# A chunked scan before a routed expert layer: another order of PE's products in a step, decay in another PSUM bank, routing in five groups

## The chip, the cores and the metric

The kernel runs on one core of a Trainium2 chip. The metric is the device time of one execution in microseconds, the median of several runs. A core has five engines that run side by side and wait for each other through semaphores: PE (matrix products into PSUM), DVE (vector), ACT (scalar functions and copies), POOL (general, and here the indirect DMAs), and SP, which here only issues DMAs. "PEld" is PE's loading of the stationary operand, which the profile lists by itself.

## The reference

Two stages. The first is a state-space scan over 4 batches x 8 heads x 768 positions, with head size 32 and state size 16:

```python
for c in range(nc):
    cum = np.cumsum(la, axis=-1)
    L = np.exp(cum[:, :, :, None] - cum[:, :, None, :]) * causal
    M = np.einsum('bhin,bhjn->bhij', Cc, Bc) * L
    y_intra = np.einsum('bhij,bhjd->bhid', M, xc)
    y_inter = np.einsum('bhin,bhnd->bhid', Cc, state) * np.exp(cum)[:, :, :, None]
    y[:, :, sl] = y_intra + y_inter
    state = decay_full[:, :, None, None] * state + np.sum(Bx, axis=2)
```

The second takes the result as 3072 tokens of 256 numbers, gives each token to the best of 8 experts (top 1 of a product with a gate matrix), and computes there `relu(x @ w1[e]) @ w2[e]`, times the gate's probability.

## The kernel before, in words

The scan works on chunks of 64 positions, two batches at a time: 24 chunks ("steps"), in two runs of 12, each run beginning with an empty state. The program is written out by hand, one loop over n from 0 to 25 at its end, and each engine does its instructions in the order in which that loop issues them. In step n the work of three chunks is under way: chunk n (its decay matrix L and its scores), chunk k = n - 1 (its state and its output y), chunk j = n - 2 (its output turned into token rows). The pieces:

- `decay(n)`: DVE's scan gives L from `abc`, a PSUM tile that `a_rows(n)` fills by one full-size product.
- `scores(n)`: 8 products of 32 rows x 64 columns into the tile g; `weigh(n)`: DVE multiplies g by L, giving M.
- `scaled_B(n)`: POOL scales B by L's last column, giving bs.
- `own(k)`: 8 products of 64 x 32 into the bank A, the chunk's part of the state; `fade(k)`: ACT scales the carried state (Sd); `state(k)`: DVE adds the two to the new state S.
- `decay_in(n + 2)`: 3 full-size products (128 x 128, bf16), copied by ACT to dec; `decayed_C(n + 2)`: POOL multiplies it with C, giving ctd.
- `y(k)`: 8 products of 32 x 64 of ctd with the carried state (y<-ctd,S), then 16 of 64 x 32 of M with x (y<-M,xn), into the tile y; ACT copies it to yT.
- `rows(j)`: full-size products of yT with an identity and the gate weights, into the tile rows_ps (tokens and their gate scores), copied by ACT.
- `masks(g)`: ACT spreads C for four chunks ahead.

An fp32 product counts as two PE instructions in the profile.

Routing works on groups of chunks (`RGS`). The first `GA` groups, 17 chunks together, are the first pass; the last 7 chunks are placed during the expert phase. When the rows of a group are complete, its choice is made in stages that later steps carry out (`due`): stage 0 `choose_max` (largest score), stage 1 `choose` (one-hot of the expert) and `count` (POOL), stage 2 `rank_pe` (small full-size products on PE that number the tokens) and `rank` (DVE). The bank of rank_pe is that of rows_ps. Then `place(k)`, an indirect DMA on POOL's queue, scatters a chunk's rows into an array in DRAM, sorted by expert; one chunk a step, from the list `todo`. `empty_consts` prepares a tile of empty rows (zrows) that SP writes behind the tokens in step 21.

At step 23 SP issues the reading of the first two experts' tokens, which waits for all scatters of the first pass. Then follow the experts: h (first product, relu on ACT), y_ps (second product), scaled and scattered to the output. Loads of inputs and of the first experts' weights are issued by SP behind counted numbers of PE products.

The order of PE in step n is: own, decay_in, rank_pe (if due), the two parts of y, scores, a_rows, rows.

Of the kernel before, what the change touches and what calls it, by code (L numbers as in the profile page):

```python
# [9 lines left out]
FP32 = mybir.dt.float32  # L10
# [11 lines left out]
CH = 64  # L22
# [4 lines left out]
NG = NT // CG  # L27
RGS = [2, 3, 3, 3, 3, 3, 7]
GA = 6
R0 = [sum(RGS[:i]) for i in range(len(RGS))]  # L30
# [14 lines left out]
def ssd_then_moe(ctx, tc, x, ad_in, az_in, B, BT, CT, w_gate, w1, w2, out):  # L45
# [94 lines left out]

    def empty_consts():

        z = sm.tile([128, 1], FP32, name="zero")
        nc.gpsimd.memset(z, 0.0)
        none_i = sm.tile([112, CAP // 112], I32, name="none_i")
        nc.gpsimd.iota(none_i, pattern=[[0, CAP // 112]], base=N, channel_multiplier=0)
        nc.scalar.copy(zrows, bc(z[0:112, 0:1, None], list(zrows.shape)))
        nc.gpsimd.tensor_copy(zrows[:, :, TOK].bitcast(I32), none_i)

    iota_i = sm.tile([128, E], I32, name="iota_i")  # L150

# [23 lines left out]
    def mm(out, lhsT, rhs, **kw):  # L175
        i = nc.tensor.matmul(out, lhsT=lhsT, rhs=rhs, **kw)  # L176
        passes[0] += 2 if rhs.dtype == FP32 else 1
        if batches and passes[0] >= 99 + 253 * sent[0] // 2:
            sent[0] += 1
            for send in batches.pop(0):  # L180
                d = send()
                tc.add_manual_dep(d.ins, i.ins.name,
                                  mybir.DependencyInfo(mybir.DependencyClass.Sync, mybir.DependencyReason.DATA),
                                  reason="behind the entry of a block")

    def empty(e):
# [99 lines left out]

    def masks(g, uu=(0, 1)):

        if "ctm" not in gr[g]:
            gr[g]["ctm"] = wk.tile([128, CG, 2, 2, CH], FP32, name="ctm")  # L290
        m = gr[g]["ctm"]
        for u in uu:
            nc.scalar.mul(m[:, :, :, u, :], gr[g]["CT"].rearrange("p (c s i) -> p c s i", c=CG, s=2), par[:, u:u + 1])  # L293

# [28 lines left out]
    def state_bank(k):  # L323

        if "A" not in st[k]:
            st[k]["A"] = ps.tile([128, 2, 128], FP32, name="A", bufs=1)
        return st[k]["A"]

    def decay_in(ns, bank):
# [33 lines left out]
    def scaled_B(n):  # L363
        if n % NC == NC - 1:
            return
        nc.gpsimd.tensor_tensor(out=bs[n % 2], in0=gr[n // CG]["B"][:, n % CG].rearrange("p (h m) -> p h m", h=8),  # L366
                                in1=bc(st[n]["L"][:, :, CH - 1:CH], [128, 8, NS]), op=ALU.mult)

    def scores(n):
        c = n % CG  # L370
        g = ps.tile([128, 2, 512], FP32, name="g", tag="g", bufs=1)
        for s in range(2):
            for t in range(2):
                for v in range(2):
                    r = slice(64 * t + 32 * v, 64 * t + 32 * v + 32)
                    o = c * 128 + s * CH
                    mm(g[64 * t:64 * t + 64, v, 128 * s:128 * s + 128],
                                     lhsT=gr[n // CG]["BT"][r, o:o + CH],
                                     rhs=gr[n // CG]["ctm"][r, c, s].rearrange("p u i -> p (u i)"),
                                     start=(s == 0), stop=(s == 1), skip_group_check=True)  # L380
        st[n]["g"] = g
# [11 lines left out]
    def own(k):  # L393
        if k % NC == NC - 1:
            return
        A = state_bank(k)
        xk = gr[k // CG]["x"][:, k % CG]

        for s in range(2):
            for t in range(2):  # L400
                for v in range(2):
                    r = slice(64 * t, 64 * t + 64)
                    h = 4 * s + 2 * v
                    mm(A[32 * (2 * t + v):32 * (2 * t + v) + 32, 0, 64 * s:64 * s + 64],
                                     lhsT=bs[k % 2][r, h:h + 2].rearrange("p u m -> p (u m)"),
                                     rhs=xk[r, h * D:(h + 2) * D], start=(s == 0), stop=(s == 1),
                                     skip_group_check=True)
# [11 lines left out]
    def state(k):  # L419
# [3 lines left out]
        new = wk.tile([128, 2, 2 * D], FP32, name="S", bufs=3)  # L423
        A = st[k]["A"][:, 0].rearrange("p (s d) -> p s d", s=2)
        for u in range(2):
# [9 lines left out]
    def y(k):  # L435
        p = ps.tile([128, 2, 512], FP32, name="y", bufs=1)
        inter = k % NC > 0
        xk = gr[k // CG]["x"][:, k % CG]
        if inter:
            for s in range(2):  # L440
                for t in range(2):
                    for v in range(2):
                        r = slice(64 * t + 32 * v, 64 * t + 32 * v + 32)
                        o = s * CH
                        mm(p[64 * v:64 * v + 64, t, s * CH:s * CH + CH], lhsT=carry[k][r, s],
                                         rhs=st[k]["ctd"][r, o:o + CH], start=(s == 0), stop=False,
                                         skip_group_check=True)
        for s in range(2):
            for q in range(4):
                for t in range(2):  # L450
                    r = slice(64 * t, 64 * t + 64)
                    o = (4 * s + q) * D
                    mm(p[D * q:D * q + D, t, s * CH:s * CH + CH], lhsT=xk[r, o:o + D],
                                     rhs=st[k]["M"][r, 4 * s + q], start=(not inter and s == 0), stop=True,
                                     skip_group_check=True)
        st[k]["yT"] = wk.tile([128, 2, 128], FP32, name="yT")
        nc.scalar.copy(out=st[k]["yT"], in_=p[:, :, 0:128])  # L457
# [4 lines left out]

    def rows(k, bank):

        p = ps.tile([128, DM + E], FP32, name="rows_ps", tag=bank, bufs=1)
        for t in range(KT):
            mm(p[:, 128 * t:128 * t + HB], lhsT=st[k]["yT"][:, t], rhs=turn[:, HB * t:HB * t + HB],
                             start=(t == 0), stop=(t == KT - 1), skip_group_check=True)
        g = grp[k]
        nc.scalar.copy(out=rt[g][:, k - R0[g], 0:DM + E], in_=p)  # L470

# [7 lines left out]
    def choose_max(g):  # L479
        n = RGS[g]  # L480
        lg = rt[g][:, :, 128:HB]
        sh = [128, n, E]
        mx = route.tile([128, RG], FP32, name="mx")[:, 0:n]
        nc.vector.tensor_reduce(mx, lg, axis=AX, op=ALU.max)
        sub = route.tile([128, RG, E], FP32, name="sub")[:, 0:n]
        nc.vector.tensor_tensor(out=sub, in0=lg, in1=bc(mx[:, :, None], sh), op=ALU.subtract)

        eq = route.tile([128, RG, E], FP32, name="eq")[:, 0:n]
        nc.vector.scalar_tensor_tensor(out=eq, in0=sub, scalar=0.0, in1=bc(rev_e[:, None, :], sh),
                                       op0=ALU.is_equal, op1=ALU.mult)  # L490
        rt_v[g] = eq

    def choose(g):
        n = RGS[g]
        sl = slice(R0[g], R0[g] + n)
        eq = rt_v[g]
        m2 = route.tile([128, RG], FP32, name="m2")[:, 0:n]
# [54 lines left out]
    def place(k):  # L552
# [8 lines left out]
        else:  # L561
            tc.declare_no_dep(s_.ins, group="la",
                              reason="places of the second pass lie behind the rows that the first one reads")
            tc.add_to_no_dep_group("pb", s_.ins)


# [212 lines left out]
    with tc.manual_schedule():  # L779
# [19 lines left out]
        late_consts(hs)  # L799
        todo, due = [], {}  # L800
        for n in range(0, NT + 2):
# [4 lines left out]
            if n < NT:  # L806
                decay(n)
            if 0 <= k < NT:
                fade(k)
                own(k)  # L810
                if n > 1 and n + 2 < NT:
                    decay_in([n + 2], state_bank(k)[:, 1:2])
                for stage, q in jobs:
                    if stage == 2:
                        rank_pe(q, ps.tile([128, RG + 1, E], FP32, name="rank", tag="rows", bufs=1))
                state(k)
                y(k)
            for stage, q in jobs:
# [8 lines left out]
            if n < NT:  # L827
                scores(n)
                scaled_B(n)
                if n > 1 and n + 2 < NT:  # L830
                    decayed_C([n + 2])
                if n + 1 < NT:
                    a_rows(n + 1)
                weigh(n)

                if c in (1, 2) and g + 1 < NG:
                    masks(g + 1, (c - 1,))
                if n in act_jobs:
                    act_jobs[n]()
                if n == 12:  # L840
                    empty_consts()
            if 0 <= j < NT:
                if n == NT + 1:
                    keep_on()
                rows(j, "A" if n == NT + 1 else "rows")
                q = grp[j]
# [3 lines left out]
                if j == R0[q] + RGS[q] - 1:  # L850
                    if q < GA:
                        for i, d in enumerate((1, 2, 3) if q == 0 else (1, 1, 2)):
                            due.setdefault(n + d, []).append((i, q))
# [19 lines left out]
            if todo:  # L873
                place(todo.pop(0))
            for stage, q in jobs:
# [157 lines left out]
```

## Time and profile before

| what | us |
| --- | --- |
| median of 3 runs | 270.06 (268.4 to 270.72) |
| the profiled execution, its own time | 271.81 |
| its span, first to last instruction | 270.0 |
| scan, from the first L (7.05) to the last rows product (about 81.2) | 74 |
| expert phase, from its first h product (83.20) | to the end |

PE's mean granted clock is 0.992. A line of the windows gives a stretch of time and the busy time of each engine in it; a line of the chain gives a start, a duration, and the work that the end of the program hung on at that time; a line of the timeline gives start, duration from the first to the last of the instructions that it merges, engine, line of the program, operation, output and inputs, number, and in brackets how long its engine stood idle before it and what ended that. "issue" there is a wait that the profile shows no cause for.

A busy PE need not be a PE at its peak, since the ends of its products are modelled. What separates two products is better read from their starts.

### The profile page before, as it was taken

To read this page: it belongs to the slowest core of one execution; us is meant where nothing else is said; L and a number is where in the kernel's file an instruction comes from. 1 tells how busy PE (TensorE), PEld (TensorE's weight loads), DVE (VectorE), ACT (ScalarE), POOL (GpSimd) and SP (SyncE) were. 2 spreads that over 40 slices of the span, in tenths; PEclk is the share of its full clock that TensorE was granted. 3 is DMA by queue.
4 is the path that set the end of the run, shared out by engine and by line. 5 is a ranking of instruction groups with operands and counts; after the bars stand their busy time and mean duration, and the time that the engine had idled before them with its cause. 6 is when DMAs were issued, how large, how long until landed. Compare 5 with 4: busy or idle time off the path is not lost.

```text
span 270.0 us, 7603 instructions
## 1 busy us (share of the span) xinstructions
PE 252.9 (94%) x3044; PEld 213.7 (79%) x3067; DVE 110.7 (41%) x358; ACT 104.5 (39%) x304; POOL 87.0 (32%) x171
## 2 busy tenths in 40 slices
PE   8799898999997999999999999999999999999990
PEld 2577677677776888888888888888998978989770
DVE  4889887888854240421211111233225115321010
ACT  6958574655543423223232323141050520604200
POOL 5666875866720002025504120202211102121021
PEclk9999999999999999999999999999999999999996
DMA  6956767671434899949695959533330601401010
GB/s 182 374 172 171 228 199 236 165 247 51 135 118 101 212 367 310 384 177 294 236 256 202 279 199 335 130 91 78 103 85 9 94 4 30 90 6 40 2 35 28
DMA packets 29715, 43.57 MB, mean 161 GB/s; under 512 B 16203, under 2 KB 19917, under 8 KB 27984
## 3 DMA queue, kind: packets, MB, share of 16 engines
q1 hardware_dynamic: 27152, 36.32, 45.4%
q0 software_dynamic: 2496, 6.41, 7.1%
q8 instruction: 36, 0.59, 0.9%
q14 instruction: 31, 0.25, 0.3%
HBM read 29.10 MB, written 10.73 MB: 147 GB/s over the span
## 4 chain that ended last, share of the span: by engine, by line
PE 82%; DVE 5%; DMA 4%; issue 4%; POOL 2%; ACT 1%; POOLq 0%; ACTq 0%; DVEq 0%
PE h_ps L685 33%; PE y_ps L720 30%; PE y L176 5%; PE rows_ps L176 4%; PE g L176 3%; PE A L176 3%; PE yh_ps L731 3%; DVE L L359 2%; DMA x_hbm<-rows,pos 1%; DMA xs<-x_hbm 1%; DMA az<-in_az_dram 1%; DMA ct<-in_CT_dram 1%; DVE M L386 1%; PE rank L176 1%; DVE S L431 1%
## 5 line engine op out<-in xcount | busy, mean ns | idle before, releaser
L685 PE MATMUL h_ps<-xT,w 128*128 128x256 f32 (+3 forms) x516 | 90.3, 334 | 0.6 <-ACT xT L641 0.5
L685 PEld LDWEIGHTS h_ps<-xT,w 128*128 128x128 f32 x516 | 81.3, 190 | 8.2 <-ACT xT L641 0.7
L720 PE MATMUL y_ps<-w,hT 128*128 128x256 f32 x384 | 84.9, 380 | 0.0
L720 PEld LDWEIGHTS y_ps<-w,hT 128*128 128x128 f32 x384 | 72.6, 190 | 10.5 <-issue 0.8
L696 ACT ACTIVATE hT<-h_ps 128x256 f32<-128x256 f32 (+3 forms) x128 | 43.3, 339 | 60.8 <-PE h_ps L685 53.1
L711 POOL DMA_INDIRECT out_dram<-yo,xs x24 | 23.7, 988 | 91.1 <-ACT yo L703 64.7
L553 POOL DMA_INDIRECT x_hbm<-rows,pos x24 | 24.4, 1015 | 20.6 <-DMA x_hbm<-zrows 13.3
L359 DVE TENSOR_TENSOR_SCAN L<-abc,ident 128x512 f32<-128x512 f32 x24 | 29.1, 1213 | 0.0
L651 DVE COPY pl<-xs 128x256 uint16<-128x256 uint16 x44 | 10.4, 298 | 43.8 <-DMA xs<-x_hbm 43.7
L658 DVE COPY xT<-plT 128x512 uint16<-128x512 uint16 (+1 forms) x30 | 10.6, 415 | 33.6 <-DMA plT<-pl 27.8
L703 ACT ACTIVATE yo<-y_ps,gate 128x256 f32<-128x256 f32 x14 | 6.6, 474 | 39.4 <-PE y_ps L720 24.5
L386 DVE TENSOR_TENSOR M<-g,L 128x512 f32<-128x512 f32 x24 | 16.5, 687 | 5.6 <-PE g L176 5.1
L176 PE MATMUL rows_ps<-turn,yT 128*128 128x136 f32 x96 | 15.4, 283 | 3.5 <-issue 2.7
L705 DVE TENSOR_SCALAR yo<-y_ps,gate 128x256 f32<-128x256 f32 x10 | 4.8, 482 | 29.3 <-PE y_ps L720 29.3
L176 PE MATMUL g<-ctm,bt 32*64 32x128 f32 x384 | 16.3, 280 | 0.5 <-ACT ctm L293 0.4
L176 PEld LDWEIGHTS rows_ps<-turn,yT 128*128 128x128 f32 x96 | 14.5, 192 | 1.3 <-issue 0.4
L711 POOL DMA_INDIRECT out_dram<-yh,xh x4 | 3.9, 978 | 35.7 <-ACT yh L733 23.9
L470 ACT COPY rows<-rows_ps 128x264 f32<-128x264 f32 x24 | 9.1, 380 | 13.5 <-PE rows_ps L176 10.9
L176 PE MATMUL y<-M,xn 64*32 64x64 f32 x768 | 12.9, 223 | 1.2 <-issue 1.2
L457 ACT COPY yT<-y 128x256 f32<-128x256 f32 x24 | 8.9, 372 | 12.2 <-PE y L176 10.2
L176 PEld LDWEIGHTS g<-ctm,bt 32*64 32x64 f32 x384 | 10.4, 131 | 3.2 <-ACT ctm L293 0.9
L366 POOL TENSOR_TENSOR bs<-bn,L 128x128 f32<-128x128 f32 x22 | 9.0, 410 | 11.1 <-DVE L L359 10.0
(132 smaller groups left out, 203.3 us busy)
## 6 DMA issues: line engine op xcount, KB each, us to landing
w<-in_w_dram SPq DMA_DIRECT2D x13, 1024.0 KB
x_hbm<-zrows SPq DMA_DIRECT2D x8, 463.8 KB
xn<-in_x_dram SPq DMA_DIRECT2D x12, 256.0 KB
w<-in_w_dram SPq DMA_DIRECT2D x12, 256.0 KB
xs<-x_hbm SPq DMA_DIRECT2D x8, 265.0 KB
ct<-in_CT_dram SPq DMA_DIRECT2D x6, 256.0 KB
bt<-in_BT_dram SPq DMA_DIRECT2D x6, 256.0 KB
bn<-in_B_dram SPq DMA_DIRECT2D x6, 256.0 KB
```

What stands on the lines that cost most here:

```text
L176: i = nc.tensor.matmul(out, lhsT=lhsT, rhs=rhs, **kw)
L359: nc.vector.tensor_tensor_scan(out=s["L"].rearrange("p h i -> p (h i)"), data0=s["abc"], data1=ident8.rearrange("p h i -> p (h i)"), initi ...
L366: nc.gpsimd.tensor_tensor(out=bs[n % 2], in0=gr[n // CG]["B"][:, n % CG].rearrange("p (h m) -> p h m", h=8), in1=bc(st[n]["L"][:, :, CH - ...
L386: nc.vector.tensor_tensor(out=s["M"].rearrange("p (s v u) i -> p s v (u i)", s=2, v=2), in0=s["g"][:, :, 0:256].rearrange("p v (s f) -> p ...
L470: nc.scalar.copy(out=rt[g][:, k - R0[g], 0:DM + E], in_=p)
L553: s_ = nc.gpsimd.indirect_dma_start(out=x_hbm[:, :], out_offset=bass.IndirectOffsetOnAxis(ap=pos[:, k:k + 1], axis=0), in_=rt[grp[k]][:, k ...
L651: nc.vector.tensor_copy(pl[:, i, :, t], f[:, :, HB * t:HB * t + 128])
L658: nc.vector.tensor_copy(xT.bitcast(U16).rearrange("p t (j c) -> p c t j", c=2), tt)
L685: nc.tensor.matmul(p[:, i:min(i + step, n)], lhsT=w[:, c:c + 128], rhs=xT[:, t, i:min(i + step, n)], start=(t == 0), stop=(t == KT - 1))
L696: nc.scalar.activation(hT[:, f, 0:n], p, func=ACT.Relu)
L711: s_ = nc.gpsimd.indirect_dma_start(out=out[:, :], out_offset=bass.IndirectOffsetOnAxis(ap=xs[:, TOK:TOK + 1].bitcast(I32), axis=0), in_=y ...
L720: nc.tensor.matmul(p, lhsT=hT[:, f], rhs=w_sb[e][1][:, f * DM:f * DM + DM], start=(f == 0), stop=(f == FT - 1))
```

## The change

Of PE's order in a step: y's part of M and x comes first, right behind own, and y's part of the carried state after it; rank_pe follows y; decay_in comes after a_rows and before rows. Its result goes no more into bank A (which shrinks to 128 columns) but into columns 128 to 256 of the first bank of y's tile. decayed_C is made for chunk n + 1 at the beginning of step n, on POOL ahead of scaled_B.

Of routing: the first pass has five groups (2, 4, 4, 4, 3) instead of six (2, 3, 3, 3, 3, 3). The comparison eq moves from stage 0 to stage 1; the three stages have a step each for the first three groups, and stages 0 and 1 share one for the last two (before, only the first group had three steps). A scatter now waits for the scores of its step (of the step before, for two scatters that are issued at the beginning of steps 19 and 21 in addition to one at each step's end).

Of the rest: masks are made in halves, one in every step, from the second group of chunks on; zrows is filled in step 20, not 12, with POOL's part at the end of the step; the last rows product has a tile of its own name in bank A.

```diff
-RGS = [2, 3, 3, 3, 3, 3, 7]
-GA = 6
+RGS = [2, 4, 4, 4, 3, 7]
+GA = 5
...
-            st[k]["A"] = ps.tile([128, 2, 128], FP32, name="A", bufs=1)
+            st[k]["A"] = ps.tile([128, 128], FP32, name="A", bufs=1)
...
     def y(k):
-        p = ps.tile([128, 2, 512], FP32, name="y", bufs=1)
+        p = st[k]["y"] = ps.tile([128, 2, 512], FP32, name="y", bufs=1)
...
+        for s in range(2):
+            for q in range(4):
+                for t in range(2):
...
+                    mm(p[D * q:D * q + D, t, s * CH:s * CH + CH], lhsT=xk[r, o:o + D],
+                                     rhs=st[k]["M"][r, 4 * s + q], start=(s == 0), stop=not inter,
+                                     skip_group_check=True)
         if inter:
...
-                                         rhs=st[k]["ctd"][r, o:o + CH], start=(s == 0), stop=False,
+                                         rhs=st[k]["ctd"][r, o:o + CH], start=False, stop=True,
...
+        def place_one():
+            d = place(todo.pop(0))
+            tc.add_manual_dep(d.ins, scored[0].ins.name,
+                              mybir.DependencyInfo(mybir.DependencyClass.Sync, mybir.DependencyReason.DATA),
+                              reason="behind a step's scores")
...
                 decay(n)
+                if n > 2 and n + 1 < NT:
+                    decayed_C([n + 1])
+                if n in (NT - 5, NT - 3):
+                    place_one()
             if 0 <= k < NT:
                 fade(k)
                 own(k)
-                if n > 1 and n + 2 < NT:
-                    decay_in([n + 2], state_bank(k)[:, 1:2])
+                state(k)
+                y(k)
                 for stage, q in jobs:
                     if stage == 2:
                         rank_pe(q, ps.tile([128, RG + 1, E], FP32, name="rank", tag="rows", bufs=1))
-                state(k)
-                y(k)
...
                 scores(n)
                 scaled_B(n)
-                if n > 1 and n + 2 < NT:
-                    decayed_C([n + 2])
                 if n + 1 < NT:
                     a_rows(n + 1)
                 weigh(n)
-
-                if c in (1, 2) and g + 1 < NG:
-                    masks(g + 1, (c - 1,))
+                if n > 1 and n + 2 < NT:
+                    decay_in([n + 2], st[k]["y"][:, 0:1, 128:256])
+
+                if g + 1 < NG:
+                    if g == 0 and c in (1, 2):
+                        mask_jobs += [lambda g=g, u=c - 1: masks(g + 1, (u,))]
+                    if g:
+                        mask_jobs += [lambda g=g, u=c // 2, i=2 * (c % 2): masks(g + 1, (u,), slice(i, i + 2))]
                 if n in act_jobs:
                     act_jobs[n]()
-                if n == 12:
-                    empty_consts()
+                if n == 20:
+                    empty_consts(0)
+                if mask_jobs:
+                    mask_jobs.pop(0)()
...
-                        for i, d in enumerate((1, 2, 3) if q == 0 else (1, 1, 2)):
+                        for i, d in enumerate((1, 2, 3) if q < GA - 2 else (1, 1, 2)):
...
             if todo:
-                place(todo.pop(0))
+                place_one()
+            if n == 20:
+                empty_consts(1)
```

## The prediction

> **What bounds the kernel now.** I read the stage windows first, then the chain of waits, then the timeline of one clean step of the scan.
>
> ```profile
> 20.00:40.00 20.00, 18.32 (x553) 14.31 (x559) 17.61 (x43) 13.91 (x40) 15.11 (x34) 1.00 0.66 200
> ...
> 60.00:80.00 20.00, 18.45 (x593) 14.64 (x589) 15.92 (x39) 10.44 (x33) 11.40 (x21) 1.00 0.32 104
> ...
> 160.00:200.00 40.00, 40.00 (x212) 35.87 (x211) 11.23 (x49) 12.24 (x37) 6.94 (x7) 1.00 0.49 138
> ```
>
> The columns are PE, PEld, DVE, ACT, POOL, clock, DMA share, GB/s. From 83 us on, in the expert phase, PE is full, and the change touches nothing there. In the scan PE is at 92%, but DVE at 80 to 88% is close behind. So PE leads the scan by little.
>
> ```profile
> 75.55 3.50 DMA x_hbm<-rows,pos
> 79.07 2.96 DMA xs<-x_hbm
> 82.08 0.67 PE xT_ps L632 x4
> ...
> 83.20 11.68 PE h_ps L685 x56
> ```
>
> The chain of waits leaves the scan by a DMA: the last token tile of the first pass is scattered at 75.55 (step 22), read back from 79.07, and the experts begin at 83.20. PE ends its own scan near 81.2 and waits 0.9 us for the read. What counts is therefore when step 22 reaches its scatter. Its scores start at 74.95 and take 0.67: end 75.62. I call the end of step n's scores G(n); the expert phase starts 7.6 us after G(22).
>
> ```profile
> 70.38 0.63 PE L176 MATMUL rows_ps<-turn,yT 128*128 128x136 f32 x4 [0.16 <-PE g L176]
> ...
> 70.94 0.43 PE L176 MATMUL A<-xn,bs 64*32 64x64 f32 x16
> 71.04 0.38 ACT L470 COPY rows<-rows_ps 128x264 f32<-128x264 f32 x1 [0.92 <-PE rows_ps L176]
> ...
> 71.30 0.34 PE L176 MATMUL A<-adp,hsel 128*128 128x128 bf16 x3
> 71.32 0.59 ACT L416 ACTIVATE Sd<-S,dec 128x64 f32<-128x64 f32 x2
> ...
> 71.57 0.46 PE L176 MATMUL y<-ctd,S 32*64 32x64 f32 x16
> ...
> 71.96 0.45 PE L176 MATMUL y<-M,xn 64*32 64x64 f32 x32
> 72.01 0.27 ACT L339 COPY dec<-A 128x128 f32<-128x128 f32 x1
> ...
> 72.31 0.47 DVE L431 SCALAR_TENSOR_TENSOR S<-A,par,Sd 128x64 f32<-128x64 f32 x2 [0.20 <-ACT dec L339]
> ...
> 72.34 0.67 PE L176 MATMUL g<-ctm,bt 32*64 32x128 f32 x16
> ...
> 73.08 0.69 DVE L386 TENSOR_TENSOR M<-g,L 128x512 f32<-128x512 f32 x1 [0.30 <-PE g L176]
> ```
>
> This is step 21; the next rows start at 73.17, so it takes 2.79 us and PE waits for nobody. The steps from 19.69 (rows of step 4) to 75.78 (step 22) average 3.12: 2.79, plus the rank products, plus gaps inside y that the chain calls "issue" (0.42 at 27.63, 0.49 at 43.70), about 3 us in all. I leave those gaps as they are.
>
> **What the Trainium skill says.** The Trainium skill, TensorEngine Tiling (Array Packing), Key Properties: a change of tiling mode, as against a change of tile, drains TensorE. The trace agrees and gives the price. Own (64*32): 16 matmuls of 222 ns end 0.43 after the first began, so the last began at +0.21; dec (128*128) begins at +0.36. The border is 0.15. The same sum gives 0.15 for dec to y<-ctd,S, 0.15 for that to y<-M,xn, 0.14 for that to g. Inside dec, one mode, matmuls start 0.06 apart. The Trainium skill, PSUM — Partial Sum Buffer, PSUM bank collisions raise a hardware error: two engines in one bank and quadrant collide even at different columns. So a bank's readers and writers must be put in order, as here: S at 72.31 waits 0.20 for ACT's copy of dec out of the same bank A (2.4 us in 5 waits over the scan).
>
> **The change, part by part.**
>
> *PE order.* From own's last start to g's first: before 4 x 0.147 of borders + 0.12 (dec) + 0.24 + 0.24 (the two y parts) = 1.19. After: 0.06 + 0.24 + 0.15 + 0.24 + 0.06 = 0.75, as own and y<-M share 64*32, and y<-ctd and g share 32*64; dec, now between abc and rows in full-size mode, adds 3 x 0.06 = 0.18. That is 0.26 less a step. Steps 2 to 21: 18 of them 0.26; steps 12 and 13, at the change of batch, 0.1 and 0.2; step 22, without dec, 0.17. Sum 5.2. The bound from below is no gain, if a join of one mode costs a drain too; from above 0.30 a step, as inside own 16 start in 0.21.
>
> *Rank.* Before, a group of three costs PE 0.30 beside dec, in one mode with it (first at 58.53, y at 58.92 instead of 58.62): six groups 1.8. After, rank stands between two 32*64 products: two borders for one join, plus six matmuls for a group of four: about 0.55, five groups 2.75. Against it stand 1.2 us that PE idled ahead of rank (30.29 to 30.82, 49.25 to 49.65, 68.20 to 68.69), since rank now comes a microsecond later. But POOL's count is later too: the scatter now starts only at G + 0.05, then 1.01, then four counts of 0.20 and a copy of 0.19: G + 2.1, and rank wants it at G + 1.85. I give back half of the 1.2. PE's sum: -5.2 + 0.9 - 0.6 = -4.9.
>
> *ACT and DVE behind the shorter step.* New step, from G: rows start +0.34, own +0.90, y<-M +1.17, y<-ctd +1.55, g +1.86, next G +2.53. Dec ends +0.6, ACT copies it by +0.86, does a half mask (0.36), then the rows copy from +1.05 to 1.2; from rows copy to the end of Sd it takes 0.87 (71.04 to 71.91): Sd at +2.0, S till +2.45, then the choice c, then M, visible 0.74 later. The next y<-M wants it at 2.53 + 1.17 = 3.70. So c up to 0.5 is free, where before, y<-M came at the next G + 1.74 and 1.3 was. Max and subtract (0.17 + 0.19 to 0.5) fit; eq, max, one-hot (3 x 0.2) miss by 0.1; the last two groups, which do both in one step, miss by 0.55 each. Sum 1.3. DVE as a whole has one group (1.4 us) less to do. ACT's casts in steps 5 and 7 (0.40; 1.04, now beside a half mask that was not there) delay the copy of y: since dec writes into y's bank, PE's dec must wait for that copy, due at G + 0.2 and done near G + 0.7 after step 7: 0.5. The zero fill (1.08) moves from step 12, which has no Sd behind it, to step 20, which has; the mask is gone there (-0.36) and a rank step is 0.55 longer: 0.15 stays, all 1.08 if that cover fails. About 2.0; inner gaps of PE cover some: 1.6.
>
> *The rest.* Masks in halves: 4 x 0.37 for 2 x 0.72, ACT idles; nothing, unless ACT is late. S no longer waits for the dec copy, but Sd takes its place. Decayed C a step later on POOL, ahead of the scaled B: 0.46 in POOL's wait for L (0.4 to 1.0); both are wanted a step later. The scatter's wait: behind it on POOL stand the count and decayed C, wanted by rank and by the step after. The two extra scatters (steps 19 and 21, 1.0 us of POOL each before scaled B) keep the last one in step 22 with groups of four; scaled B is then ready near G + 2.9, wanted at G + 3.4. SP's queue keeps its order; its triggers count PE passes, whose number a step is the same. The last scatter began 0.07 before G(22) and now begins 0.05 after: +0.1. The expert weights lie ahead: PE waits 1.4 us for all of the phase's inputs, and its later loads are triggered by the phase itself.
>
> Sum: -4.9 + 1.6 + 0.1 = -3.2 us. Made against a span of 270.0 in an execution of 271.81, which is 1.75 above the median of 270.06; laid on the median: **266.9 us**.
>
> **The rivals.**
> 1. *PE's gain stays whole* (c hidden by POOL no longer slowing DVE: a subtract takes 0.51 beside POOL, 0.18 without): -4.9, rank's waits gone, 264.8. For it: DVE has a group less. Against: the 0.5 of cover.
> 2. *ACT and DVE take over the step.* If Sd comes 0.25 later than I put it (each ACT operation counted at its full record, without the 0.1 of overlap between neighbours), every masked step misses by 0.1 to 0.3 and the choice steps by more: 4 of 4.9 are eaten, 269.2, within 1%. For it: DVE was at 88% from 20 to 40.
> 3. *The shared bank makes it slower.* PE's dec stands at the head of PE's queue, with rows, own and both y parts behind it, and waits for ACT's yT copy; the next y<-M waits for ACT's dec copy. In a plain step yT is copied by G + 2.4 and dec wants it at 2.53 + 0.2: 0.3 to spare. From a slip of 0.3 + 0.26 in most steps on (ACT runs Sd just before yT), a step loses more than the borders gave: a slip of 0.8 costs 0.5 - 0.26 = 0.24 in each of 20 steps, +4.8, 274.9. For it: the copies of dec came 0.6 late in places (53.51, for matmuls over by 52.9). Against it: ACT is busy 0.5 to 0.7 of the time, and the durations would have to be 0.8 longer in sum than the rows show.
> 4. *Nothing changes, as a hidden stretch moved*: if the read back or the weights set the expert start. Against it: the scatter follows the step by queue order. 270.
>
> **How the numbers follow.** About 1% (2.7 us) is what a measurement of this kernel can tell from no change: the bounds are 267.4 and 272.8. My forecast (-2 to -4.2) 0.48, of which a quarter lies short of 2.7; rival 1 0.17; rival 2 0.23; rival 3 0.08; rival 4 0.04. Faster: 0.36 + 0.17 = 0.53, slower 0.08, within 1% the rest, 0.39. Range 264.3 to 270.3: it leaves out rival 3 and the far half of rival 1.
>
> **What the profile will show.** Right: own, y<-M, y<-ctd in this order, y<-M some 0.06 after own's last start and g as close to y<-ctd, clean steps near 2.53; last scatter near 72 us, experts near 80. DVE's S waits for Sd, not dec. Wrong: a border of 0.15 at the joins (then rival 4's time); PE idle ahead of dec with ACT's yT as its releaser (rival 3); PE idle ahead of y<-M with DVE's M in most steps, not in two to six (rival 2). A weight load that PE waits for in the expert phase would break the premise that the phase only shifts.

## The result, and the profile after

The changed kernel takes 278.43 us (median of 6 runs, 275.88 to 281.44), the kernel before 270.46 beside it: a ratio of 1.029, with an interval of 1.023 to 1.035. It is slower by 8 us where 3 us less was forecast. The medians hold every execution, while the ratios leave out those that took over 1.5% longer than the fastest of the same kernel. The profiled execution has a span of 276.4 us against 270.0.

The stage windows of the changed kernel first (columns as before: PE, PEld, DVE, ACT, POOL, clock, DMA share, GB/s):

```profile
20.00:40.00 20.00, 15.78 (x531) 13.07 (x538) 15.78 (x37) 12.66 (x40) 12.67 (x33) 1.00 0.60 182
60.00:80.00 20.00, 17.05 (x567) 13.97 (x567) 17.03 (x44) 11.47 (x37) 15.42 (x33) 1.00 0.44 144
160.00:200.00 40.00, 40.00 (x187) 35.20 (x187) 9.50 (x44) 9.90 (x28) 6.93 (x7) 1.00 0.52 157
```

From 20 to 40 us PE falls from 18.3 to 15.8 of 20, and DVE, ACT and POOL fall with it. No engine took over; all of them stood still at times. The expert phase is as full as before, so the loss lies in the scan. A clean step looks as forecast (timeline of PE, from one rows product to the next):

```profile
55.91 0.68 PE L178 MATMUL rows_ps<-turn,yT 128*128 128x136 f32 x4
56.53 0.35 PE L178 MATMUL A<-xn,bs 64*32 64x64 f32 x9
...
56.75 0.55 PE L178 MATMUL y<-M,xn 64*32 64x64 f32 x28
57.23 0.38 PE L178 MATMUL y<-ctd,S 32*64 32x64 f32 x9
...
57.51 0.62 PE L178 MATMUL g<-ctm,bt 32*64 32x128 f32 x14
58.28 0.33 PE L178 MATMUL y<-adp,hsel 128*128 128x128 bf16 x3 [0.16 <-ACT yT L467]
58.45 0.34 PE L178 MATMUL rows_ps<-turn,yT 128*128 128x136 f32 x1
```

It takes 2.54 us (55.91 to 58.45) against 2.79, and the products of equal mode run into each other without a border. Yet the scan is longer. One place shows why (timeline of PE, step 13, the first of the second run of chunks, which has no carried state):

```profile
46.62 0.41 PE L178 MATMUL y<-M,xn 64*32 64x64 f32 x17
50.12 0.33 PE L178 MATMUL y<-M,xn 64*32 64x64 f32 x11 [3.10 <-issue]
```

PE stops in the middle of one product, among matmuls whose M and x had been complete since its first: for 3.10 us from the modelled end of the matmul ahead, or 3.3 with the weight loads counted, as all such gaps are below. No data can be late there, and the profile names no releaser. The page's costliest groups, which list the idle time ahead of a group last, give the same product before and after:

```profile
L176 PE MATMUL y<-M,xn 64*32 64x64 f32 x768 | 12.9, 223 | 1.2 <-issue 1.2
```

```profile
L178 PE MATMUL y<-M,xn 64*32 64x64 f32 x768 | 15.0, 230 | 8.3 <-issue 7.2
```

What PE waited for is found among the transfers. These are the queues in two stretches of that gap, 46.8 to 47.6 and 47.6 to 48.7 (packets, MB, share of 16 engines):

```profile
q1 hardware_dynamic: 123, 0.22, 72.5%
q0 software_dynamic: 31, 0.10, 32.0%
```

```profile
q0 software_dynamic: 59, 0.15, 36.6%
q1 hardware_dynamic: 27, 0.03, 8.6%
q8 instruction: 1, 0.02, 5.2%
```

First the engines of the DMA are full of loads (q1) and of the scatter (q0); only behind them comes one packet of the queue "instruction" (q8), 16 KB, from 47.69 to 48.61 by the trace's records. PE goes on at 50.12, 1.5 us after it has landed. Counted through the trace, PE's gaps of this kind stand at instruction 193 of each 256, weight loads, matmuls and semaphores together. In the changed kernel there are seven, at 14.1, 18.9, 27.5, 32.8, 37.8, 46.8 and 80.9 us, of 1.64, 0.49, 0.33, 1.92, 0.84, 3.31 and 2.31 us: 10.8 in sum. In the kernel before 0.44 (14.81) and 0.21 (18.55) are certainly of it, and perhaps the 0.64 at 27.41: 0.7 to 1.3. (The last stands at that count, but its packet had landed at 25.35, 2.7 us before PE went on.)

The Trainium skill has a section on this, Runtime: NRT & Kernel Launch, Instruction fetch mechanics: each engine's instructions are refilled "in **16 KiB blocks** (256 instructions)" through a DMA queue of the engine's own while the current block runs. I did not use it in the prediction. The trace agrees on the size and the 256. It does not agree that the cost of a crossing is "mostly hidden".

The stalls seem to have a second cost. Behind the longest of them and behind the last one PE's granted clock is at half for 3.4 us (windows, columns as above), and the same rows product, at full clock in step 12 and at half in step 13, takes almost twice as long (timeline of PE):

```profile
50.98:54.39 3.41, 3.08 (x75) 2.72 (x72) 2.30 (x4) 1.53 (x5) 2.72 (x8) 0.50 0.68 210
85.11:88.52 3.41, 3.03 (x54) 2.55 (x56) 0.02 (x1) 1.09 (x3) 0.00 (x0) 0.50 0.48 150
```

```profile
45.79 0.68 PE L178 MATMUL rows_ps<-turn,yT 128*128 128x136 f32 x4
51.70 1.22 PE L178 MATMUL rows_ps<-turn,yT 128*128 128x136 f32 x4
```

The block of 256 instructions that PE goes on with at 50.12 lasts 5.97 us. In e1 below, the same program but for the times of its loads, that block runs at full clock from 46.38 to 50.93, 4.55. In the kernel before the clock is full until 265.8 us. From the end of the last stall to the experts' first product the changed kernel takes 6.77 us (83.23 to 90.00), e5 below, also the same but for its loads and at full clock there, 5.84. An estimate from these: 1.4 and 0.9, or 2.3 us in the two stretches.

At the end of the scan the last such stall hits the chain of waits directly (chain of the changed kernel):

```profile
80.87 0.25 PE y L178 x20
81.13 2.10 issue
83.23 0.62 PE y L178 x15
...
89.11 0.45 PE xT_ps L640 x4
...
90.01 2.02 PE h_ps L693 x12
```

The experts begin at 90.01 instead of 83.20, 6.8 us later, and from there on both run alike.

### The profile page after: what moved, and what is told of

Its sections match the earlier page's. It is cut to its first block, busy times and chain, and to the rows that moved or that the text cites. A ratio compares the mean times of both kernels' runs of the same rounds, so it can differ in the third digit from the quotient of the medians.

```text
span 276.4 us, 7661 instructions
## 1 busy us (share of the span) xinstructions
PE 250.6 (91%) x3043; PEld 213.7 (77%) x3065; DVE 109.6 (40%) x351; ACT 104.7 (38%) x312; POOL 87.5 (32%) x170
## 4 chain that ended last, share of the span: by engine, by line
PE 83%; issue 6%; ACT 4%; DVE 3%; POOL 1%; POOLq 0%; ACTq 0%; DVEq 0%
PE h_ps L693 32%; PE y_ps L728 29%; PE y L178 8%; PE rows_ps L178 3%; PE yh_ps L739 3%; PE g L178 2%; PE wake_ps L178 2%; PE A L178 2%; DVE M L395 1%; ACT yT L467 1%; PE rank L178 1%; DVE L L366 1%; ACT Sd L425 1%; ACT dec L346 1%; POOL out_dram L719 1%
## 5 line engine op out<-in xcount | busy, mean ns | idle before, releaser
L178 PE MATMUL y<-M,xn 64*32 64x64 f32 x768 | 15.0, 230 | 8.3 <-issue 7.2
L178 PEld LDWEIGHTS y<-M,xn 64*32 64x32 f32 x768 | 10.5, 109 | 9.8 <-issue 8.3
L178 PE MATMUL g<-ctm,bt 32*64 32x128 f32 x384 | 17.7, 277 | 0.5 <-ACT ctm L296 0.2
L178 PE MATMUL rows_ps<-turn,yT 128*128 128x136 f32 x92 | 16.8, 308 | 0.2 <-ACT yT L467 0.2
L178 PEld LDWEIGHTS rows_ps<-turn,yT 128*128 128x128 f32 x92 | 13.2, 203 | 0.3 <-issue 0.2
L178 PEld LDWEIGHTS g<-ctm,bt 32*64 32x64 f32 x384 | 11.7, 131 | 1.7 <-ACT ctm L296 0.8
L178 PE MATMUL A<-xn,bs 64*32 64x64 f32 x352 | 9.6, 226 | 3.3 <-issue 1.7
```

## The experiments

**T1**: the packets of PE's instructions come late because they queue behind bulk loads. The loads are triggered by counts of PE's products, "behind the entry of a block", and the new order no longer suits them. **T2**: the shared bank, PE's decay product waiting for ACT's copy of y. **T3**: the choice in three steps, the zero fill, the scatter behind the scores. "Stalls" below is the sum of gaps over 0.3 us at instruction 193 in the profiled execution. Ratios are against the kernel before on the same chip; the five sets of runs (e, f with e5, g, h with i, j) were on five chips. A run has 4 to 6 executions, f2 and i2 have 20, g2 11.

| run | median | before | ratio, interval | span profiled | stalls |
| --- | --- | --- | --- | --- | --- |
| changed kernel | 278.43 | 270.46 | 1.029 (1.023 to 1.035) | 276.4 | 10.8 |
| e1 sends later | 276.83 | 268.98 | 1.025 (1.016 to 1.034) | 272.1 | 9.1 |
| e2 before, sends earlier | 274.9 | 268.98 | 1.020 (1.013 to 1.028) | 274.6 | 8.5 |
| e3 old routing | 275.19 | 268.98 | 1.022 (1.015 to 1.029) | 274.8 | 9.2 |
| e4 old order | 272.54 | 268.98 | 1.001 (0.991 to 1.011) | 267.9 | 1.6 |
| f1 pairs | 277.45 | 271.21 | 1.020 (1.014 to 1.025) | 277.2 | 2.8 |
| f2 fill in 12 | 272.45 | 271.21 | 1.005 (1.003 to 1.008) | 270.3 | 2.5 |
| f5 pairs, fill in 12 | 277.98 | 271.21 | 1.022 (1.012 to 1.031) | 275.0 | 4.0 |
| e5 one load at a time | 274.85 | 271.21 | 1.014 (1.009 to 1.018) | 271.6 | 3.4 |
| g1 changed again | 278.14 | 269.92 | 1.036 (1.026 to 1.045) | 273.8 | 8.2 |
| g3 fill in 12, old order | 275.54 | 269.92 | 1.020 (1.010 to 1.030) | 273.5 | 1.3 |
| g4 fill in 12 again | 276.74 | 269.92 | 1.024 (1.015 to 1.032) | 275.2 | 9.4 |
| i1 mixed batches | 273.98 | 270.29 | 1.011 (1.001 to 1.021) | 271.2 | 6.9 |
| i2 the same, old routing | 274.09 | 270.29 | 1.012 (1.008 to 1.016) | 271.3 | 6.0 |
| j1 i1, empty rows later | 276.14 | 271.94 | 1.014 (1.010 to 1.019) | 272.8 | 2.9 |
| j2 j1, cast in step 8 | 275.63 | 271.94 | 1.011 (1.007 to 1.016) | 273.9 | 1.4 |

### The triggers moved, in both kernels

e1 alters one number of the changed kernel, e2 the same number of the kernel before:

```diff
-        if batches and passes[0] >= 99 + 253 * sent[0] // 2:
+        if batches and passes[0] >= 149 + 253 * sent[0] // 2:
```

```diff
-        if batches and passes[0] >= 99 + 253 * sent[0] // 2:
+        if batches and passes[0] >= 74 + 253 * sent[0] // 2:
```

> The changed kernel, with one number altered: each batch of bulk loads is triggered 50 PE passes (about 100 PE instructions, some 1 us) later. T1 (PE's own instruction packets, one of 16 KB for each 256 instructions, land late because they queue behind bulk loads whose triggers no longer suit the new order): most of the 10.8 us of PE stalls without a releaser go, down to 3 us or so, and the time falls from 278.4 to 266 to 271. T2 (the shared bank: PE's decay product waits for ACT's copy of y): no effect, 277 to 280. T3 (choice in three steps, zero fill, scatter behind the scores): no effect, 277 to 280.

> The kernel before, with its bulk loads triggered 25 PE passes (about 50 PE instructions, 0.5 us) earlier, so that they start ahead of a block's entry and not behind it. T1: PE stalls without a releaser grow from 3 us by 4 to 10 us, in the middle of products; 274 to 281. T2 and T3: neither the bank nor the choice is touched, so within 1.5 us of the kernel before, 269 to 272.

e2 shows that the times of the loads alone can do this. Nothing of the change is in it, and it loses 5.9 us, as T1 said and neither T2 nor T3. Its stalls stand at instruction 193, ten of them, and in whichever product that falls, as here in g (timeline of PE):

```profile
43.99 0.43 PE L176 MATMUL g<-ctm,bt 32*64 32x128 f32 x5
45.46 0.65 PE L176 MATMUL g<-ctm,bt 32*64 32x128 f32 x11 [1.03 <-issue]
```

In e2's stalled blocks the packet starts 1.9 to 3.5 us after the entry into the block ahead of it. Without loads (h1 below, from 21 to 74 us) it starts at most 1.4 us after. In the stalled blocks of all these runs it takes 0.9 to 2.1 us to land, and PE goes on 1.1 to 1.6 us after that. With 1.4, 1.0 and 1.3 us a block of 256 has to last 3.7 us. From 18 to 69 us a block lasts 4.0 us on the mean in e1 (eleven blocks of the new order, 3.4 to 4.9), stalls not counted, and 4.25 in e2 (the old order, 3.6 to 4.9). So there is little room, and the faster order has less of it.

e1 was a miss. The triggers 50 passes later did not bring the packets in time; nine blocks stalled, for 0.5 to 2.3 us, 9.1 us in sum. That later loads run into the packet of the next block instead is my reading; e2 shows only that their place against the block's entry counts.

### One part undone at a time

e3 puts back the routing of before, e4 the order of PE and the bank:

```diff
-RGS = [2, 4, 4, 4, 3, 7]
-GA = 5
+RGS = [2, 3, 3, 3, 3, 3, 7]
+GA = 6
```

```diff
                 own(k)
+                if n > 1 and n + 2 < NT:
+                    decay_in([n + 2], state_bank(k)[:, 1:2])
+                for stage, q in jobs:
+                    if stage == 2:
+                        rank_pe(q, ps.tile([128, RG + 1, E], FP32, name="rank", tag="rows", bufs=1))
                 state(k)
                 y(k)
```

> The changed kernel with the routing of before: six groups (2, 3, 3, 3, 3, 3), eq in the first stage, stages 0 and 1 in one step from the second group on, no scatter waiting for scores and no extra scatters; the new order of PE, decay in y's bank, the masks and the zero fill at step 20 stay. T1: the stalls belong to the order's block entries against the load triggers and stay, if moved, 273 to 280. T2: the bank stays, 276 to 280. T3: the loss goes, 266 to 270.

> The changed kernel with PE's old order in a step (own, decay, rank, y's carried part, y's M part, scores) and decay in bank A; five groups, choice in three steps, scatter behind the scores, half masks and zero fill at step 20 stay. T1: fewer semaphore instructions of PE, blocks entered nearly as in the kernel before, stalls of 3 to 5 us, 269 to 274. T2: the loss goes, 269 to 271. T3: the loss stays and the order's gain is missing, 279 to 284.

With the new order and the old routing the stalls stay (9.2); with the old order and the new routing they go (1.6). So it is the order that makes the packets late. T3's forecasts for e3, 266 to 270, and for e4, 279 to 284, fell. By time alone e4 does not part T1 from T2 (269 to 271): two of its executions took 269.62 and 269.94, two 275.14 and 275.95, of which one of the first pair was profiled. There the stalls decide, and what held up the longer two is not known. e4 also shows what the new routing costs under the old order, where rank comes early in a step (timeline):

```profile
64.68 1.01 POOL L560 DMA_INDIRECT x_hbm<-rows,pos  x1 [0.17 <-issue]
...
65.72 0.76 POOL L513 TENSOR_TENSOR cnt<-cnt,oh_all 128x8 bf16<-128x8 bf16 x3
...
66.53 0.17 PE L178 MATMUL rank<-cnt,ones_bf 128*128 128x8 bf16 x1 [2.12 <-POOL cnt L513]
```

POOL counts only behind an additional scatter, and PE's rank waits 2.1 us for the count. In the changed kernel rank comes after y, and no such wait is seen.

### The loads spaced otherwise, and the fill back in step 12

```diff
-        batches += [order[i:i + 3] for i in range(0, len(order), 3)]
+        batches += [order[i:i + 2] for i in range(0, len(order), 2)]
...
-        if batches and passes[0] >= 99 + 253 * sent[0] // 2:
+        if batches and passes[0] >= 124 + 253 * sent[0] // 2:
```

```diff
-                if n == 20:
+                if n == 12:
                     empty_consts(0)
...
-            if n == 20:
+            if n == 12:
                 empty_consts(1)
```

The first is f1, the second f2, both together f5. e5 sends one load at a time, with `99 + 253 * sent[0] // 6`.

> The changed kernel with its bulk loads sent in batches of two and not three (the same 253 PE instructions between batches, so each block of 256 PE instructions has 0.5 MB beside it and not 0.75), 25 PE passes later behind a block's entry. T1 (the new order uses up a block in 4.1 us instead of 4.5, its successor's packet starts 1.1 to 1.3 us after the entry, takes 0.9 and is usable 1.4 us after its end, 3.4 to 3.6 in all, so that it can bear a delay of 0.5 us at most, which three loads of some 1 us each exceed): the stalls between 14 and 65 us fall from 9 us to 2 or less, the one near 80 us stays; 268 to 272. Rivals (bank, choice, zero fill): 277 to 280, as none of these is touched.

> The changed kernel with the empty rows filled in step 12, as before, and not in step 20. T1: SP can write the empty rows some 1.5 us sooner, so that they lie ahead of the packet for the last block of the scan; the stall of 2.3 us near 80.9 shrinks to under 1, and 0.5 us of ACT's work goes from the chain of step 20: 275 to 277. T3 (the fill is a main cause of the loss): 272 or less. If the writes collide with the packet in another way: 278 to 280.

> Both edits together, pairs of loads 25 passes later and the fill in step 12. T1: 266 to 270, under the kernel before. T2 (bank): 276 or more.

> The changed kernel with its bulk loads sent one at a time, three in each 253 PE instructions, evenly (first trigger as in the changed kernel): the bytes are the same, but a packet of instructions can find at most one load of some 1 us before it. T1, if the depth of the queue counts: no stall above 1 us until 65 us, 270 to 274. T1, if the number of bytes per block counts whatever their spacing: 275 to 280. Rivals: 277 to 280.

f1: the stalls between 14 and 65 us fell to 1.7, as T1 said, but the time did not follow. Two loads a block take more blocks, and the last weights left at 80.7 us, in the way of the handover: the last scatter took 5.5 us to land, the tokens' reading began at 82.25, and PE waited for it from 83.4 to 86.70. The clock was then at half from 86.33 to 93.16, and the expert phase, where PE is full, took 188.9 us instead of the 186.4 of the changed kernel. f5 missed its 266 to 270 by 8 us: in it the chain runs through SP's sending of weights at 82.3 and 82.6, ahead of the reading in its queue. e5 has no stall above 1 us, as T1 said if the depth of the queue counts, though its time is 0.9 over that range and 0.15 short of the other reading's 275 to 280. f2 came out better than T1 put it, 272.45, 0.5% over before and 0.45 us over T3's "272 or less", and its stalls had gone in places ahead of step 12, where the program is unchanged. That called for a control.

### The same programs on another chip

> The changed kernel itself, once more, beside the three below on one chip. T1 (packets of instructions behind bulk loads, decided by the exact times of loads and block entries): 276 to 281, with stalls at PE instruction 193 of a block as in its first profile, 6 us or more between 12 and 65 us. If the place of the fill decides it alone, the same. If it is the chip's state and not the program: 271 to 274, near the version with the fill in step 12.

> The changed kernel with the fill in step 12, once more, to stand on the same chip as the three above. T1: 271 to 274 as before, with stalls at 193 under 4 us in sum; the difference to the changed kernel 4 us or more. If the earlier difference was the chip's and not the fill's: within 1.5 us of the changed kernel.

> The changed kernel with the fill in step 12 and with the routing of before (six groups, old stages, scatters without the wait): what is left of the change is PE's order, the decay in y's bank and the half masks. T1: if the packets come in time, PE's order alone saves what was forecast for it, and 266 to 269; if they don't, stalls at instruction 193 and 272 to 277. T2 (bank): PE's decay product waits for y's copy in more than five steps, 271 or more without stalls at 193.

> The changed kernel with the fill in step 12 and PE's old order (decay in bank A): what is left is the five groups, the choice in three steps, the scatter behind the scores, the half masks. T1: a block takes 4.5 us again and bears a later packet, 267 to 271, stalls at 193 under 3 us in sum. T3 (the new routing itself costs): 272 or more, with waits of DVE, POOL or PE's rank and none at 193.

g4 is f2 once more, instruction for instruction, and it takes 276.74 instead of 272.45; beside it the changed kernel takes 278.14. So on this chip the fill is worth 1.4 us by the medians, within the spread of either, and not 6. The rest of f2's gain goes with the chip; the changed kernel itself was not run on the chip of the f runs, so that the fill is worth more there is not excluded. The two traces show the difference at the same product. f2, then g4 (timeline of PE, step 13):

```profile
47.30 0.42 PE L178 MATMUL y<-M,xn 64*32 64x64 f32 x22
47.87 0.33 PE L178 MATMUL y<-M,xn 64*32 64x64 f32 x7
```

```profile
47.86 0.41 PE L178 MATMUL y<-M,xn 64*32 64x64 f32 x17
50.71 0.45 PE L178 MATMUL y<-M,xn 64*32 64x64 f32 x11 [2.44 <-issue]
```

The packet for this block started 0.87 us after the entry in f2 and 4.76 us after it in g4. The stalls are 2.5 us in one and 9.4 in the other, a difference of 6.9 of which 4.9 appears in the spans. In g4 the clock is at half from 33.6 to 40.4 and from 50.7 to 54.1, in f2 nowhere before 265 us. A program that lives on this edge is decided by tenths of a microsecond. g2 (fill in 12, old routing) is not in the table: its runs spread from 269.54 to 279.68, with a ratio of 1.007 (1.001 to 1.012), and decide nothing here. g3, with the old order again, has 1.3 us of stalls, as T1 said, but waits 2.3 us for the count at rank and 2.5 us for the tokens: the time is T3's. Part of it is the clock, at half behind each of these waits, from 68.6 to 72.0 and from 85.6 to 89.1; the expert phase took 188.6 us. So waits of another kind are followed by it too.

### Without loads in the middle

The pair h1 (kernel before) and h2 (changed kernel) takes the bulk loads away:

```diff
+        for g in range(2, NG):
+            gr[g].update({t: gr[g % 2][t] for t in ("CT", "BT", "B", "x")})
+        for go in w_loads(0) + w_loads(1)[0:4]:
+            go()
```

> The kernel before, without bulk loads in the middle of the scan: the inputs of the third to sixth group of chunks are not loaded (those of the first two are used in their place, so the output is another), and the weights that belong to the batches are all sent ahead of the first step. T1: packets of instructions come in time, the stalls at instruction 193 (2 to 3 us) go, 266 to 269. Rivals: no packet matters, so no change but what DMA contention cost elsewhere, 269 to 271.

> The changed kernel with the same edit (inputs of four groups not loaded, weights ahead of the first step). T1: no stall at 193 between 25 and 65 us, and the predicted saving of the new order appears against the same edit of the kernel before: 2 to 5 us less than it, 263 to 267. T2 and T3 (bank, choice, zero fill): the changed kernel stays behind the kernel before by 4 us or more, 272 or more.

The times themselves, 325.47 and 327.56, say nothing: the expert phase grows by over 50 us, probably because the repeated inputs crowd tokens onto few experts. I had not foreseen that, and the forecasts in us fell with it. The scans can be compared. With the weights sent ahead, both stall early (3.3 and 4.0 us before 22 us); from 22 to 75 us h1 has no stall over 0.3, h2 two of 0.52 and 0.92, and at the end, beside the writing of the empty rows, 1.72 and 2.20. Plain steps take 2.79 in h1 and 2.54 in h2. From the rows of step 6 to those of step 22 h1 needs 46.95 us and h2 47.74; less the stalls 46.95 and 46.3. To the experts' begin, less the stalls, 54.8 and 52.6. So with packets in time the change saves 0.7 us until step 22. The 2.1 in all is an upper bound, as h1's clock, and not h2's, is at half from 80.59 to 84.00; one rows product late in the scan, in h1 and then in h2 (chain):

```profile
82.70 1.20 PE rows_ps L176 x4
```

```profile
83.02 0.66 PE rows_ps L178 x4
```

h2 also has a late packet with no load near it, the one ahead of its stall of 0.92. The block before it was entered at 43.70, the packet started at 46.56. These are all the transfers from 44.4 to 45.8, and from 45.8 to 46.56:

```profile
q0 software_dynamic: 2, 0.00, 0.1%
```

```profile
q0 software_dynamic: 47, 0.14, 50.2%
```

For 1.4 us the DMA engines were free and the packet did not start; then a scatter came first. Loads ahead of it in the queues are thus not the only thing that makes it late.

### Towards a version that keeps the gain

i1 has pairs for the 20 input loads and threes for the weights, with the offset of f1 and the fill in 12; i2 has the old routing besides. j1 holds the empty rows back, and j2 also moves a cast of ACT:

```diff
-            if n == 21:
+            if n == 22:
                 for e in range(2):
-                    empty(e)
+                    d = empty(e)
+                    tc.add_manual_dep(d.ins, scored[0].ins.name,
```

```diff
-                 7: lambda: (term(b), term(c, half[0])), 10:
+                 7: lambda: term(b), 8: lambda: term(c, half[0]), 10:
```

> The changed kernel with the fill in step 12, the 20 input loads in pairs and the 12 weight loads in threes, all 25 PE passes later. T1: stalls at 193 under 3 us until 65 us as in the version with pairs alone, and the last weights are sent near 66 us, not at 80, so that the reading of the first tokens no longer stands behind them in SP's queue: 267 to 271. If the packets are late whatever the batches: 274 to 279.

> The same with the routing of before (six groups, old stages, scatters without the wait). T1: 266 to 270. If five groups in three steps are worth something under the new order: 1 us or more behind the version above; if they cost: 1 us or more ahead of it.

> The version with mixed batches and the fill in step 12, with the writing of the empty rows held back until the scores of step 22 (some 1.5 us after a block's entry, so that the packet of the scan's last block goes first). T1: the stall of 3.6 us near 74 us falls under 1 us, 269.5 to 272 against 274.0 of that version. If the stall there has another cause: it stays, 273 to 275. If the tokens' reading then waits for the empty rows: the experts begin no earlier, 273 to 275, with the wait in front of xT_ps and none at 193.

> The same, and in addition one of ACT's two casts of step 7 goes to step 8. T2 (the part of it that all profiles of the new order show, PE's decay product 1.0 us behind ACT's copy of y after step 7's casts): that wait falls to 0.5 or less, and the time by 0.5 to 1.0 against the run before. If the wait is only moved to step 8: no difference.

i1 missed its range by 3 us. Until 65 us its stalls were 2.6 us in sum, as forecast, and the stretch from the rows of step 6 to those of step 22 took 48.33 us, 1.8 less than in the kernel before (50.10, on another chip). Then one stall undid it (timeline of PE):

```profile
74.14 0.46 PE L178 MATMUL y<-M,xn 64*32 64x64 f32 x23
77.97 0.31 PE L178 MATMUL y<-M,xn 64*32 64x64 f32 x6 [3.37 <-issue]
```

The block ahead of it was entered at 71.59, the empty rows were sent at 71.81 and 72.74, and the packet started only at 75.53. j1 sends them at 77.51, and the stall there falls to 1.1 us, but the time, 276.14, is outside all its forecasts. Beside the empty rows the last scatter now takes 4.6 us to land (4.9 in j2; 3.50 in the kernel before), the tokens are read behind it, and PE waits for them, 1.1 us in j1 and 1.6 in j2. On this chip PE also stands still for 0.6 us in three places beside the first scatter of a group, as in f2. i2 is equal to i1 and misses its 266 to 270 as well, so five groups or six make no difference that these runs show. In j2 the wait of PE for ACT's y after step 7 falls to 0.2 (0.7 in j1). The medians differ by 0.5, within the spread; its experts begin 0.5 us earlier, but its clock is at half from 86.4 to 89.8 and the expert phase takes 188.0 us, against 186.4 in j1. None of these versions is ahead of the kernel before.

## Why the prediction was wrong

Right:
- The step of PE. Forecast: 2.79 becomes 2.53, "own and y<-M share 64*32, and y<-ctd and g share 32*64". Measured: 2.54 in clean steps of the changed kernel, 2.54 against 2.79 in the pair without loads. The Trainium skill's distinction (TensorEngine Tiling (Array Packing), Key Properties) between a change of tile and a change of tiling mode held again: the first of these joins shows no border.
- The waits at the shared bank and at the choice are few and in the forecast places: PE's decay product waits for yT once, 0.94 at 32.23 after ACT's casts of step 7, where 0.5 was forecast; the choices of the late groups cost 0.4 to 0.7 each at 61.8, 70.4 and 71.3. Rival 3, a slip at the bank in most steps, did not come about. It gave the right sign for the wrong reason.

Mis-sized: "Sum 1.3 ... About 2.0; inner gaps of PE cover some: 1.6". The waits in the changed trace come to some 3 us, the zero fill's share among them (0.4 and 0.8 at 76.3 and 77.3 for the forecast 0.15). The pair without loads saves 0.7 until step 22 and at most 2.1 in all, not 3.2. One sum is also a little off: the three intervals of idling ahead of rank make 1.4, not 1.2, which moves the forecast by 0.1. This alone would have left the change faster or even.

Failed: the step "**gaps inside y that the chain calls "issue" (0.42 at 27.63, 0.49 at 43.70), about 3 us in all. I leave those gaps as they are**", together with "SP's queue keeps its order; its triggers count PE passes, whose number a step is the same". The gaps had no cause in my account, and so I had no reason to hold them constant. Some are packets of instructions that come late. The triggers' own reason in the program, "behind the entry of a block", says what they are set for: the number of passes in a step did stay the same, but not the time that a block lasts nor the load that stands before its packet. The term that was put at 0 measured 10.8 less 0.7 to 1.3, or some 9.5 to 10. With the forecast -3.2 this gives +6.3 to +6.9; the spans differ by 6.4. The fit is in part luck: the half clock behind the stalls adds an estimated 2.3, and the saving was smaller than 3.2, so the stalls must cover 3 us or more of other waits.

What stays open: why the new order's packets start so late. e4 and e3 differ little in when the loads are sent after an entry (0.5, 0.9 and 1.4 us in e4, 0.7, 1.0 and 1.5 in e3, both for the block entered in step 11), yet the packet starts 1.4 us after the entry in e4 and 4.6 in e3. That it starts only when the loads are through is seen in the trace; why they are ahead of it is not, and h2's packet was late with free engines and no loads. Chips differ in how often this happens, and the runs don't say by what. Nor do they say why PE stands still for some 0.6 us beside the first scatter of a group on two of the chips, and in the kernel before at 27.41 and 43.49; those gaps are not at instruction 193, the one at 27.41 possibly excepted.

## What to carry to other kernels

An idle gap with no releaser is a cost with an unknown cause, not a constant: look which queue ends shortly before it, the instruction queue too, and count the engine's instructions to it. Where transfers are triggered by counts of an engine's instructions, a change of that engine's order or speed is a change of the transfers, and the time of 256 instructions against the time of a packet has to be worked out anew. Look at the granted clock behind every long standstill before pricing it, since the standstill may not be its whole cost. A saving per instruction on an engine that issues fast shortens the very time that its next instructions have to arrive in.

## What was not expected of the hardware

- PE needed the packet that was started after the entry of the block just ahead: 0.9 to 2.1 us for 16 KB, and then 1.1 to 1.6 us from its landing to PE's next instruction. The section of the Trainium skill quoted above gives PE room for 2048 instructions; the stalls at block after block, ten in e2, look like no more than two blocks of 256.
- Each stretch of half clock up to the experts' begin, and in f1, g3 and j2 just behind it, lasted 3.4 or 6.8 us and began during a standstill of PE (neither a matmul nor a weight load running) of 1.4 us or more, or within 2.1 us of its end. Five traces (the kernel before, e2, e5, f2, j1) had no standstill over 1.1 us from 10 us to the experts' begin, and no such stretch. Not each long standstill was followed by one: those of 2.1 us that ended at 66.5 in e4 and at 82.9 in e3 were not. In f1, g3 and j2 alone the clock was at half inside the expert phase before its end; it took 188.0 to 188.9 us there and 186.2 to 186.8 in the other traces with all loads. No run tests what sets the clock.
- One program, the fill in step 12, took 272.45 us on one chip (20 runs, 271.49 to 274.53) and 276.74 on another (4 runs, 274.85 to 281.49), while the kernel before took 271.21 and 269.92 there.
